# FNet mixing and gated conv FFN on one core: the order of folds and first-stage DFTs for batches 2 to 5

## The chip, the cores and the metric

The kernel runs on one core of a Trainium2 chip. The metric is the device time of one execution in microseconds, as the median of ten runs. The engines are TensorE (PE, with weight loads as PEld), VectorE (DVE), ScalarE (ACT), GpSimd (POOL) and SyncE (SP, which only issues DMAs here). Each engine works through its own queue in order; semaphores join the queues.

## The reference

Input x is (8, 3136, 256) in float32. The result feeds a gated feed-forward layer with d_ff = 1024.

```python
X = np.fft.fft(x, axis=1)
X = np.fft.fft(X, axis=2)
x = X.real                                  # (8, 3136, 256)
h = np.maximum(x @ w_in, 0.0)               # (8, 3136, 1024)
conv_out = sum(conv_w[k] * shifted(h, k - 1) for k in range(3))   # along the sequence, zero-padded
out = (h * sigmoid(conv_out)) @ w_out       # (8, 3136, 256)
```

## The kernel before

The DFT along the sequence is done per batch. First VectorE **folds** the input: sums and differences of mirrored quarters of the sequence and of mirrored features, so that a quarter of the table suffices. `fold_ops(b)` returns fourteen such operations, seven for each half `h` of a batch: `pair(0)`, `pair(2)`, `both(6)`, `feats(1)`, `both(4)`, `evens`, `feats(0)`. They work in place on a buffer `xh` (two buffers, one per half) and put their results into `wt[b]` (tiles `w`). `feats` also has a small copy and a memset on POOL. The input reaches `xh` by `load_ops`: one plain DMA and, for half 1, three tiny ones, all issued by SP, and four indirect DMAs issued by POOL for the mirrored rows. A load for a buffer waits until the last fold on that buffer is done.

Then the **first DFT** of the batch runs as eight units (`units(b)`). A unit is four matmuls of `w` with a table into one PSUM tile `pd` (`Unit.matmuls`, shown as eight matmul instructions in the profile), a copy of half of it by ScalarE (`copy`, L287 and L306; two of the units have none) and a finishing pair of VectorE operations (`fin`, L291/L294, L310/L312, L322/L324), which write the transformed batch `PQ[b]` (tiles `pt` and `qt`). There is one `pd` buffer, so a unit's first matmul waits for the pair of the unit ahead of it.

The rest is a pipeline over 256 **steps**: for each batch four chunks of the sequence, for each chunk eight blocks of 128 of the 1024 hidden features. So `per` is 32 steps for a batch. The step loop at the end of the function writes all queues by hand. In step t:

- TensorE: the two products of step t+1 into `pb` and `pa` (second DFT and `w_in` in one), then `mm2` of step t-3 with `w_out` into `po` (twelve instructions, fourteen at some steps), then what `side` holds for "pe".
- ScalarE: the sigmoid of step t-2 (L711), the copies of `pb` of step t+1 (L675), what `side` holds for "act", the seed of `pa` for step t+2 (L641), the first tap of step t (L692).
- VectorE: `combine` of step t (two of L686), what `side` holds for "dve", two taps of step t-1 (L698), the gate of step t-2 (L719, and L721 at some steps).
- POOL: its half of the gate (L718), a memset at some steps, and the loads in `side`.
- SP: the loads in `side` under "load", and the output stores, which fall due every eighth step.

`mm2` of step t-3 needs the gate that VectorE wrote in its step t-1. `combine` of step t needs the products of TensorE's step t-1.

The work on coming batches is put into steps by `at(step, where, fn)`. The list `ends` sets it: the folds of batch b are spread evenly over the steps `ends[b-1]` to `ends[b]`, and its first DFT over `ends[b]` to 32b-3. Before, `ends` is [9, 20, 46, 72, 98, 125, 157, 189]. Batch 1's DFT has nine steps (20 to 28, its last finishing pair in step 29), batch 2's fifteen, batch 3's twenty-one, batch 4's twenty-seven, the later ones thirty-two. A fold is not put where its step is in the set `taken`; that set holds the steps with a finishing pair, and two with another VectorE operation.

```python
    ends = [9] + [max(26 * b - 6, per * (b - 1) - 3) for b in range(1, B)]
...
            at(cs[i + 1], "act", u.copy)
            at(cs[i + 1], "dve", u.fin)
            taken.add(cs[i + 1])
...
        cs = [free(c0 + j * n // len(ops)) if b > 1 else c0 + j * n // len(ops) for j in range(len(ops))]
```

Finishing pairs are entered into `side` before folds, so where both fall into one step the pair comes first in VectorE's queue. When a half's last fold is placed, the loads of the next batch's same half go into the steps behind it, one operation a step.

Of the kernel before, what the change touches and what calls it, by code (L numbers as in the profile page):

```python
# [38 lines left out]
def kernel(  # L39
# [11 lines left out]
    B, S, D = x.shape  # L51
# [411 lines left out]
    def spread(b, cs):  # L463

        for c in cs:
            ch = chunks[c]
            eb[b, c] = ebp.tile([P, HN], F32, name="eb", tag="eb")[:, 0:ch.k1 - ch.k0]
            nc.sync.dma_start(out=eb[b, c], in_=ed[b:b + 1, ch.k0:ch.k1].to_broadcast([P, ch.k1 - ch.k0]))
# [322 lines left out]
    per = len(chunks) * NF  # L791
    side = {}

    def at(cycle, where, fn):
        side.setdefault((cycle, where), []).append(fn)
# [9 lines left out]
        at(NF + 1 + j // 3, "load", fn)  # L805


    ends = [9] + [max(26 * b - 6, per * (b - 1) - 3) for b in range(1, B)]
    taken = set()

    def free(cycle):

        while cycle in taken:
            cycle += 1
        taken.add(cycle)
        return cycle
# [13 lines left out]
    for b in range(1, B):  # L830
        begin, us, *_ = units(b)
        us = us[0:4] + us[5:]
        c0, n = ends[b], per * b - 3 - ends[b]
        at(max(c0, per * (b - 1) + 1), "pe", begin)
        cs = [c0 + i * n // len(us) for i in range(len(us) + 1)]
        for i, u in enumerate(us):
            k = cs[i + 1] - cs[i]
            for j in range(k):
                at(cs[i] + j, "pe", lambda u=u, j=j, k=k: u.matmuls(j, k))
            at(cs[i + 1], "act", u.copy)  # L840
            at(cs[i + 1], "dve", u.fin)
            taken.add(cs[i + 1])
        at(cs[-1] - 2, "load", lambda b=b: spread(b, range(len(chunks) - 1)))
        at(per * b + 1, "load", lambda b=b: spread(b, [len(chunks) - 1]))
    for b in range(1, B):
        ops = fold_ops(b)
        c0, n = ends[b - 1], ends[b] - ends[b - 1]
        cs = [free(c0 + j * n // len(ops)) if b > 1 else c0 + j * n // len(ops) for j in range(len(ops))]
# [107 lines left out]
```

## Time and profile before

| | us |
|---|---|
| median of ten runs | 1223.79 (1222.27 to 1224.17) |
| the profiled execution, its own time | 1223.55 |
| its span, first to last instruction | 1221.8 |

| engine | busy, us | share of the span |
|---|---|---|
| PE | 1187.1 | 97% |
| PEld | 905.4 | 74% |
| DVE | 1126.1 | 92% |
| ACT | 877.0 | 72% |
| POOL | 371.2 | 30% |

Times are microseconds unless marked ns. L719 is line 719 of the kernel. A matmul is pipelined, and its recorded end is modelled: the next one starts before it. A stage's row gives its start and end, its length, and for each engine the busy time with the number of instructions, then the granted TensorE clock, the DMA engines' busy share and GB/s. In a list of waits, a row gives who waited for whom, the sum, the count and the longest. In a timeline, a row gives start and duration, and in brackets the idle time of the engine before it with what ended it.

### The profile page before, as it was taken

The page shows a single profiled execution, that of the slowest core. Times are in us where ns is not written, and L with a number is a line of the kernel's source. Part 1 is how long each engine was busy: PE and PEld are TensorE (multiplying, and loading weights), DVE is VectorE, ACT ScalarE, POOL GpSimd, SP SyncE. Part 2 cuts the span into 40 slices and gives each one's busy share as a digit, 9 for nine tenths or more (in the row PEclk, how much of TensorE's full clock was granted, in tenths as well). Part 3 has the DMA queues.
Part 4 walks back from the last instruction along what each step waited for, and adds up shares of the span by engine and source line. Part 5 has one row for each costly group of instructions (what it writes and reads, how often), then busy time and mean ns, then how long its engine had stood idle before and what let it go on. Part 6 is the DMA issues. An engine that isn't in the chain of part 4 may idle for free.

```text
span 1221.8 us, 15450 instructions
## 1 busy us (share of the span) xinstructions
PE 1187.1 (97%) x4876; PEld 905.4 (74%) x4876; DVE 1126.1 (92%) x1696; ACT 877.0 (72%) x1832; POOL 371.2 (30%) x474
## 2 busy tenths in 40 slices
PE   5999999999999999999999999999999999999998
PEld 4676677667777777677777777777777787777776
DVE  7799978998999999999999999999998888899996
ACT  2467666777667777777776777777777777788884
POOL 5224532244142413242324242232222122222222
PEclk9999999999999999999999999999999999999999
DMA  9512231112031211211112020310001000110000
GB/s 237 178 8 80 81 48 59 54 55 75 4 99 44 73 52 33 75 53 53 53 58 61 18 79 27 86 47 26 27 1 53 31 26 27 46 33 27 26 27 31
DMA packets 70213, 66.30 MB, mean 54 GB/s; under 512 B 28123, under 2 KB 57827, under 8 KB 70131
## 3 DMA queue, kind: packets, MB, share of 16 engines
q1 hardware_dynamic: 64493, 52.18, 14.9%
q0 software_dynamic: 5120, 12.85, 3.4%
q8 instruction: 39, 0.64, 0.2%
q14 instruction: 43, 0.35, 0.1%
q10 hardware_dynamic: 518, 0.28, 0.1%
HBM read 39.53 MB, written 25.74 MB: 53 GB/s over the span
## 4 chain that ended last, share of the span: by engine, by line
PE 68%; DVE 22%; issue 4%; ACT 2%; DMA 1%; DVEq 0%; SPq 0%; ACTq 0%
PE po L94 42%; PE pb L94 10%; PE pa L94 10%; DVE g L698 7%; PE pd L94 7%; DVE h L686 4%; DVE g L719 3%; DVE xh L158 2%; DVE xh L169 1%; ACT nb L675 1%; DVE w L186 1%; DVE w L187 1%; DVE xh L173 0%; DMA xh<-in_x_dram 0%; DVE pt L291 0%
## 5 line engine op out<-in xcount | busy, mean ns | idle before, releaser
L94 PE MATMUL po<-wout,g 128*128 128x256 f32 x3072 | 709.8, 381 | 13.9 <-DVE g L719 13.3
L94 PEld LDWEIGHTS po<-wout,g 128*128 128x128 f32 x3072 | 577.9, 190 | 170.0 <-DVE g L719 50.8
L698 DVE SCALAR_TENSOR_TENSOR g<-h,cw,g 128x770 f32<-128x770 f32 (+1 forms) x512 | 549.0, 1072 | 9.3 <-ACT g L692 0.2
L718 POOL TENSOR_TENSOR g<-g,h 128x385 f32<-128x385 f32 (+1 forms) x256 | 232.5, 908 | 781.4 <-ACT g L711 520.3
L711 ACT ACTIVATE g<-g 128x385 f32<-128x385 f32 (+2 forms) x512 | 244.4, 527 | 196.8 <-DVE g L698 194.2
L675 ACT ACTIVATE nb<-pb 128x386 f32<-128x386 f32 (+2 forms) x472 | 208.2, 494 | 85.9 <-PE pb L94 85.1
L686 DVE CUSTOM_DVE_ANT_0 h<-pa,nb 128x386 f32<-128x386 f32 (+2 forms) x492 | 255.6, 560 | 3.7 <-ACT h L672 3.7
L692 ACT ACTIVATE g<-h,cw 128x770 f32<-128x770 f32 (+1 forms) x256 | 243.5, 951 | 0.1
L94 PE MATMUL pb<-qt,G 127*128 127x387 f32 (+2 forms) x512 | 212.7, 496 | 0.0
L94 PE MATMUL pa<-pt,G 128*128 128x387 f32 (+2 forms) x512 | 211.8, 494 | 0.0
L641 ACT ACTIVATE pa<-eb,ge 128x387 f32<-128x387 f32 (+2 forms) x252 | 151.7, 602 | 1.3 <-PE pa L94 0.7
L94 PEld LDWEIGHTS pa<-pt,G 128*128 128x128 f32 x512 | 96.8, 189 | 73.6 <-issue 18.2
L719 DVE TENSOR_TENSOR g<-g,h 128x385 f32<-128x385 f32 (+1 forms) x256 | 146.2, 571 | 0.9 <-ACT g L711 0.9
L94 PE MATMUL pd<-tab,w 98*128 98x196 f32 (+3 forms) x448 | 122.4, 374 | 0.0
L133 POOL DMA_INDIRECT xh<-in_x_dram,idx x64 | 106.8, 1669 | 13.4 <-issue 9.6
L94 PEld LDWEIGHTS pb<-qt,G 127*128 127x128 f32 x512 | 94.5, 190 | 17.6 <-issue 0.9
L94 PEld LDWEIGHTS pd<-tab,w 98*128 98x128 f32 (+1 forms) x448 | 83.9, 190 | 12.6
L738 ACT COPY os<-po 128x256 f32<-128x256 f32 x196 | 57.6, 394 | 8.5 <-PE po L94 4.6
L158 DVE TENSOR_TENSOR xh<-xh 98x1020 f32<-98x1020 f32 (+1 forms) x32 | 40.9, 1283 | 2.7 <-DMA xh<-in_x_dram,idx 2.5
L169 DVE TENSOR_TENSOR xh<-xh 98x1024 f32<-98x1024 f32 (+1 forms) x32 | 42.0, 1314 | 0.1
L291 DVE TENSOR_TENSOR qt<-as,pd 128x197 f32<-128x197 f32 (+1 forms) x14 | 7.2, 516 | 21.6 <-ACT as L287 21.6
L291 DVE TENSOR_TENSOR pt<-as,pd 128x197 f32<-128x197 f32 (+1 forms) x14 | 7.3, 520 | 20.2 <-ACT as L287 20.2
(114 smaller groups left out, 404.2 us busy)
## 6 DMA issues: line engine op xcount, KB each, us to landing
out_dram<-os SPq DMA_DIRECT2D x192, 128.0 KB
xh<-in_x_dram SPq DMA_DIRECT2D x16, 784.0 KB
eb<-ed SPq DMA_DIRECT2D x16, 193.5 KB
tab<-dft_seq_dram SPq DMA_DIRECT2D x4, 589.5 KB
raw<-in_moe_w_in_dram SPq DMA_DIRECT2D x4, 512.0 KB
raw<-in_moe_w_out_dram SPq DMA_DIRECT2D x1, 2048.0 KB
eb<-ed SPq DMA_DIRECT2D x8, 209.0 KB
eb<-ed SPq DMA_DIRECT2D x8, 193.0 KB
```

The costliest lines, as they stand in the source:

```text
L94: nc.tensor.matmul(o, l, r, start=start, stop=stop, skip_group_check=True)
L133: nc.gpsimd.indirect_dma_start(out=xh[b, h][0:NP, 7 - m].rearrange("p q d -> p (q d)"), out_offset=None, in_=bass.AP(tensor=x.tensor, offs ...
L158: vt(a[:, :, :, 1:D], a[:, :, :, 1:D], r[:, :, :, D - 1:0:-1], op=ALU.add)
L641: act(pa[s][:, 0:n], eb[b, c], AF.Copy, scale=ge[:, f:f + 1])
L675: act(nb[s][:, i, cols], p[:, cols], AF.Copy, scale=-1.0 if i else 1.0)
L686: nc.vector._custom_dve(TENSOR_ADD_SAT, out=to, in0=a[:, cols], in1=c[:, i, cols], s0=BIG, s1=0.0)
L692: act(gs[s], hs[s][:, 0:n], AF.Copy, scale=cw[:, 0, s[2]:s[2] + 1])
L698: stt(out=g, in0=h[:, k:k + n], scalar=cw[:, k, f:f + 1], in1=g, op0=ALU.mult, op1=ALU.add)
L711: act(gs[s][:, c], gs[s][:, c], AF.Sigmoid)
L718: gt(g[:, p], g[:, p], h[:, p], op=ALU.mult)
L719: vt(g[:, v], g[:, v], h[:, v], op=ALU.mult)
L738: nc.scalar.copy(out=osb[:, j % 2], in_=pt[:, j % 2])
```

## The change

`ends` gets other values: [9, 20, 36, 61, 93, 125, 157, 189]. The folds of batch 2 lie in steps 20 to 35, those of batch 3 in 36 to 59, those of batch 4 in 62 to 90, and those of batch 5 in 94 to 122. The first DFT of batch 2 takes steps 36 to 60, that of batch 3 steps 61 to 92, that of batch 4 steps 93 to 124. The finishing pairs of batch 1 no longer keep folds out of their steps, so that six steps from 21 to 26, and step 29, hold a pair and a fold. The loads move with the folds. `taken` is otherwise as before.

```diff
-    ends = [9] + [max(26 * b - 6, per * (b - 1) - 3) for b in range(1, B)]
+
+    ends = [9, 20, per + 4] + [per * (b - 1) - 3 for b in range(3, B)]
...
-            taken.add(cs[i + 1])
+            if b > 1:
+                taken.add(cs[i + 1])
```

## The prediction

> **What bounds the kernel now.** I read the page's busy times first, then the stages, then the waits and the timeline inside the stages that stood out.
>
> ```profile
> PE 1187.1 (97%) x4876; PEld 905.4 (74%) x4876; DVE 1126.1 (92%) x1696; ACT 877.0 (72%) x1832; POOL 371.2 (30%) x474
> PEclk9999999999999999999999999999999999999999
> ```
>
> TensorE looks full and VectorE nearly so. The granted clock is flat, so no stage is slow for that reason. But a po matmul takes 381 ns in the records while the next starts 216 ns later, so "busy" hides pauses. I therefore marked TensorE's steps by their first pb product (step 20 at 151.42 us, 28 at 196.86, 36 at 234.34, 61 at 351.75, 93 at 497.43, 125 at 642.41, 157 at 785.28, 189 at 927.69) and asked for those stretches:
>
> ```profile
> 151.42:196.86 45.44, 44.81 (x189) 34.79 (x188) 35.79 (x58) 28.63 (x60) 10.93 (x12) 1.00 0.36 62
> 196.86:234.34 37.48, 35.89 (x149) 26.08 (x149) 36.76 (x61) 26.69 (x56) 9.09 (x17) 1.00 0.11 36
> 234.34:351.75 117.41, 114.59 (x469) 87.30 (x468) 111.06 (x168) 84.29 (x175) 41.11 (x45) 1.00 0.20 60
> 351.75:497.43 145.68, 144.02 (x590) 109.89 (x589) 138.24 (x212) 107.06 (x223) 49.02 (x61) 1.00 0.18 57
> 497.43:642.41 144.98, 142.44 (x581) 108.17 (x581) 138.18 (x212) 107.41 (x223) 46.64 (x58) 1.00 0.17 55
> 642.41:785.28 142.87, 142.58 (x590) 110.37 (x589) 134.79 (x208) 108.16 (x224) 45.27 (x56) 1.00 0.16 50
> 785.28:927.69 142.41, 141.44 (x581) 108.71 (x581) 134.62 (x209) 108.30 (x224) 38.41 (x53) 1.00 0.12 38
> ```
>
> Columns: length, then busy time of PE, PEld, DVE, ACT, POOL. In the first stretch (steps 20-27) VectorE is idle for 9.65 of 45.44 us, in the second (28-35) for 0.72 of 37.48. So the bound changes from TensorE to VectorE within sixteen steps. The reason is where the folds lie. The same stretches with the instructions on xh alone:
>
> ```profile
> 151.42:196.86 45.44, 1.30 (x1) 1.00 0.36 62
> 196.86:234.34 37.48, 7.88 (x10) 1.00 0.11 36
> 234.34:351.75 117.41, 19.77 (x23) 1.00 0.20 60
> 351.75:497.43 145.68, 24.05 (x28) 1.00 0.18 57
> 497.43:642.41 144.98, 21.41 (x26) 1.00 0.17 55
> 642.41:785.28 142.87, 18.59 (x22) 1.00 0.16 50
> ```
>
> A batch's folds are 22 instructions, 18.6 us. Steps 20-27 have one of them; the stretches behind carry 23, 28 and 26. What this costs is in TensorE's wait list for steps 28 to 46 and in one step's timeline:
>
> ```profile
> PEld po L94 <- DVE g L719: 11.7, 13, 1.3
> ```
> ```profile
> 245.41 1.02 DVE L686 CUSTOM_DVE_ANT_0 h<-pa,nb 128x385 f32<-128x385 f32 x2
> 245.55 2.46 PEld L94 LDWEIGHTS po<-wout,g 128*128 128x128 f32 x12 [1.11 <-DVE g L719]
> ```
>
> TensorE has its two products out (1.30 us), then waits for the gate L719 of VectorE's step before. A VectorE step with a fold takes about 4.6 us, without one 3.4; TensorE's is 3.89 (12 po x 0.216 + 4 products x 0.325), plus a DFT's 13.3 spread over its steps. In steps 21-27 it is the other way round, VectorE waits:
>
> ```profile
> 171.10 0.33 ACT L287 COPY as<-pd 128x197 f32<-128x197 f32 x1
> 171.47 0.52 DVE L291 TENSOR_TENSOR qt<-as,pd 128x197 f32<-128x197 f32 x1 [2.76 <-ACT as L287]
> ```
>
> **The change, part by part.** The order of instructions confirms the moves; all matmuls stay. The first DFT remains in steps 20-28. Batch 2's fourteen folds go from steps 20-44 to 20-35, its DFT from 46-60 to 36-60; batch 3's folds from 46-70 to 36-59, its DFT from 72-92 to 61-92; batches 4 and 5 follow (starts 98 to 93 for DFT 4). From step 130 on nothing differs.
>
> *Steps 20-27.* Six folds (about 1.25 us each) enter steps 21-26. They stand behind the DFT's finishing pair in VectorE's queue, so the 2.76 us idle ahead of that pair are not filled; the slack behind it is what counts. Walk a step: the copy ends about 1.99 after TensorE's step begins (169.38 to 171.43 in the timeline), the pair takes 0.78, fold 1.25, two taps and gate 2.33: gate at +6.35. The next mm2 can start at 5.35 (TensorE's mean step here) + 1.30 = +6.65. That holds by 0.3. Going step by step from VectorE's 158.09 at step 21, the gates come 1.4, 1.2, 0.0, 0.1, 1.4 and 1.2 us ahead of need. Where VectorE is not waiting it has 3.38 + 0.8 + 1.25 = 5.4 to TensorE's 5.4. Cost 0.1. No row shows pair and fold in one step, so bounds: at least 0, since TensorE pauses there for only 0.9, in step 20; at most all six on the path, 6 x 1.25 = 7.5. I take 0.1, since each piece has its row.
>
> A rule speaks against this. When POOL's gate ran at 97.46-98.33, the fold begun at 97.62 took 1.780, its twin behind it 1.208. The Trainium skill (GPSIMD Engine Reference, 1. Specifications) says that POOL's SBUF interfaces are shared with VectorE, with contention for instructions that have two SBUF inputs, as each fold has. By the rule six folds grow by 0.57, 3.4 us, and with 0.3 slack a step the stretch loses about 2. By the rows at steps 36-40, also with gate and indirect loads, folds took 1.26 to 1.32; and behind the finishing pair the gate has mostly run. I keep 1.25, and 2 us in the range.
>
> *Steps 28-35.* VectorE is the bound and gets seven folds for six (the new one beside the DFT's last finishing pair): +1.3, minus 0.1 slack. Sum to step 36: +1.3.
>
> *Steps 36-60.* Folds 23 to 22 instructions, and the DFT's 13.3 us on TensorE now spread over all 25 steps. TensorE's own work is 25 x 3.89 + 13.3 + 1.3 for the wider last chunk of a batch = 111.8, so 5.6 of the 117.4 are pauses. In the two stretches that already have this layout the same sum gives 140.8 and 139.1: pauses of 2.1 and 3.3. Here the load of VectorE on TensorE is like theirs (111.1 less 1.3 for one fold is 109.8, over 111.8 is 0.98; there 134.8/140.8 and 134.6/139.1 are 0.96 and 0.97), so I take 2.9: -2.7.
>
> *Steps 61-92 and 93-124.* They become copies of 125-156 and 157-188, with equal TensorE work: 145.68 to 142.87, and 144.98 to 142.41: -2.8, -2.6. The fold time agrees: 5.5 and 2.9 us leave VectorE.
>
> A second reading of these three: the Trainium skill (Perfetto Trace Analysis, Identifying the Most-Contended Engine) wants TensorE's headroom judged by the share of weight loads, not of matmuls. Shares are 0.744, 0.754, 0.746 before, 0.773 and 0.763 in the target stretches. At 0.768, 0.773 and 0.763 they would take 113.7, 142.2 and 141.8: -10.3 instead of -8.1. I stay with the step sums, since the share also counts missing records.
>
> *Queues.* Batch 3's loads move from steps 36-50 to 27-41, batch 4's from 59-75 to 47-65, batch 5's less. On SP a load waits for the buffer's last fold (53.3 us in 8 waits, longest 13.3); behind it are stores and eb loads, due three or more steps later. POOL's indirect loads take 1.0-3.1 us each with POOL busy 10.9 of 45.4. Batch 2's second half landed at 184.8 and would be read at 197.8; later ones have nine steps. Cost nothing; if a landing slipped beyond 13 us, the fold at step 28 would pay the rest.
>
> Sum: 1.3 - 2.7 - 2.8 - 2.6 = -6.8. The profiled execution took 1223.55 (span 1221.8), so 1216.75; it lies 0.24 under the median 1223.79, so 1217.0.
>
> **Rivals.** (A) The above, 72%: with errors of about 1 in each term, 1214.5 to 1219.5.
> (B) Bunching: folds at neighbouring steps (36/37, 40/41, 43/44, two of 4.6 us) still make TensorE wait, and the rule on shared interfaces holds early: +2.5 -1.0 -2.8 -2.0 = -3.3, 1220.5. For it: L719 waits now sit at just such pairs. Against: steps 125-188 have pairs too. 12%, a third of it within 0.2% of no change, 2.45 us, which is about what a measurement of this kernel can tell.
> (C) More: steps 20-35 free, pauses of 2.1 per 32 steps everywhere: -3.9 -2.8 -3.8 = -10.5, 1213.3. Against: 28-35 has no VectorE slack. 7%.
> (D) Slower: the folds in steps 21-26 stand behind the finishing pair's wait, and that chain, not TensorE, sets the step. Then none of the idle time is usable and the moved folds are paid whole: 7 x 1.25 = 8.7, plus 6 x 0.5 of contention = 11.7, less 8.1 later: +3.6, 1227.4. It decides from about 8.1 lost in 20-35, 1.2 per fold. For it: the margin is only 0.3 a step. Against: past the margin only the excess is paid, not the fold. 7%, with 2% for a smaller such loss near no change.
>
> Faster by over 0.2%: 72 + 8 + 7 less some tail of A: 84%. Same 9%, slower 7%. The range 1213.5 to 1221.2 covers A, nearly all of B and the edge of C.
>
> **What would show it.** Right: VectorE busy near 42-43 us in steps 20-27 with that stretch's length within 0.5 of 45.4; step 36 about 1.3 later than 234.34; the PEld wait on L719 in steps 28-46 down from 11.7 to under 8; steps 61-92 and 93-124 within 1 us of 142.9 and 142.4. Wrong: L719 waits appearing in steps 21-27 (D), folds there at 1.7 us (the rule), a DMA as releaser of L158 at step 28, or pauses of 5 us staying in 36-60 (B).

## The result and the profile after

| | before | after |
|---|---|---|
| median | 1223.69 us (28 runs) | 1218.71 us (8 runs, 1217.69 to 1218.91) |
| ratio | | 0.9959, 95% interval 0.995 to 0.9967 |
| profiled execution, its span | 1223.55, 1221.8 us | 1218.81, 1217.0 us |

The change saves 5.0 us; 6.8 had been forecast. The stages of the changed kernel, cut at the same steps as before (length, then busy time of PE, PEld, DVE, ACT, POOL):

```profile
151.72:197.64 45.92, 45.08 (x190) 34.71 (x188) 42.27 (x68) 28.27 (x60) 12.93 (x16) 1.00 0.36 58
197.64:236.71 39.07, 35.98 (x149) 25.97 (x149) 38.34 (x62) 26.68 (x56) 16.45 (x21) 1.00 0.25 79
236.71:352.42 115.71, 114.58 (x469) 87.06 (x468) 110.18 (x166) 83.83 (x175) 39.24 (x44) 1.00 0.20 60
352.42:495.30 142.88, 142.59 (x589) 110.41 (x589) 134.65 (x208) 108.38 (x224) 45.96 (x56) 1.00 0.16 51
495.30:637.67 142.37, 141.41 (x582) 108.74 (x582) 134.59 (x209) 108.31 (x224) 45.40 (x57) 1.00 0.17 52
```

The instructions on xh alone, in the first three of these:

```profile
151.72:197.64 45.92, 8.88 (x11) 1.00 0.36 58
197.64:236.71 39.07, 9.09 (x11) 1.00 0.25 79
236.71:352.42 115.71, 18.58 (x22) 1.00 0.20 60
```

The folds went where the diff says: 11 instructions in each of the first two stages, 22 in the third. VectorE is busy for 42.27 us in steps 20-27, where it had been for 35.79. Against the prediction:

| steps | before | after | difference | forecast |
|---|---|---|---|---|
| 20-35 | 82.92 | 84.99 | +2.07 | +1.3 |
| 36-60 | 117.41 | 115.71 | -1.70 | -2.7 |
| 61-92 | 145.68 | 142.88 | -2.80 | -2.8 |
| 93-124 | 144.98 | 142.37 | -2.61 | -2.6 |
| sum | | | -5.04 | -6.8 |

Step 20 starts 0.30 us later in this profile, and nothing moves behind step 125, which gives the spans' -4.8. Steps 20 to 60 together won nothing (+0.37); the whole gain came from 61 to 124. TensorE's wait list for steps 28 to 46 says where the first two rows fell short:

```profile
PEld po L94 <- DVE g L719: 9.7, 11, 2.6
```

Before it was 11.7 us in 13 waits. The waits are two fewer now, but one is of 2.6 us, where the longest had been 1.3. It comes in step 30, behind the step that holds a finishing pair and a fold at once. The timeline from VectorE's step 29 on:

```profile
203.25 0.99 ACT L711 ACTIVATE g<-g 128x448 f32<-128x448 f32 x2 [1.64 <-DVE g L698]
...
204.15 0.91 ACT L675 ACTIVATE nb<-pb 128x418 f32<-128x418 f32 x2
204.94 0.32 ACT L287 COPY as<-pd 128x196 f32<-128x196 f32 x1
...
205.30 0.52 DVE L291 TENSOR_TENSOR pt<-as,pd 128x196 f32<-128x196 f32 x1 [0.48 <-ACT as L287]
...
206.00 1.22 DVE L158 TENSOR_TENSOR xh<-xh 99x1020 f32<-99x1020 f32 x1
...
209.94 0.92 PE L94 MATMUL po<-wout,g 128*128 128x256 f32 x3 [1.93 <-DVE g L719]
```

This is the chain that the prediction's walk did not have. ScalarE starts with the sigmoid, which waits for VectorE's taps (L698); then come the two copies of pb, and only then the pair's copy. TensorE's DFT unit had ended at 202.50, 2.4 us before that copy began. So when VectorE is late, ScalarE is late with it, and the pair waits for a copy that hangs on VectorE's own last step. The same in step 24:

```profile
175.78 0.94 ACT L711 ACTIVATE g<-g 128x385 f32<-128x385 f32 x2 [2.68 <-DVE g L698]
...
176.62 0.91 ACT L675 ACTIVATE nb<-pb 128x418 f32<-128x418 f32 x2
177.42 0.32 ACT L287 COPY as<-pd 128x196 f32<-128x196 f32 x1
...
177.77 0.51 DVE L291 TENSOR_TENSOR qt<-as,pd 128x196 f32<-128x196 f32 x1 [0.56 <-ACT as L287]
```

VectorE's step began at 176.21, where the gate of the step before ended, and the pair at 177.77: 1.56 us later, of which the last 0.56 were idle. Combine alone would have let it start at 1.0.

### The profile page after: what moved, and what is told of

Read it like the earlier page. It is cut to its first block, busy times and chain, and to the rows that moved or that the text cites. A ratio compares the mean times of both kernels' runs of the same rounds, so it can differ in the third digit from the quotient of the medians.

```text
span 1217.0 us, 15448 instructions
## 1 busy us (share of the span) xinstructions
PE 1185.7 (97%) x4876; PEld 906.6 (74%) x4876; DVE 1125.2 (92%) x1696; ACT 877.7 (72%) x1832; POOL 372.8 (31%) x474
## 4 chain that ended last, share of the span: by engine, by line
PE 69%; DVE 21%; issue 4%; ACT 2%; DMA 1%; DVEq 0%; SPq 0%; ACTq 0%
PE po L94 43%; PE pb L94 10%; PE pa L94 10%; DVE g L698 7%; PE pd L94 6%; DVE h L686 3%; DVE g L719 3%; DVE xh L158 2%; ACT nb L675 1%; DVE xh L169 1%; DVE w L186 1%; DVE w L187 1%; DMA xh<-in_x_dram 0%; DVE xh L173 0%; DVE pt L291 0%
## 5 line engine op out<-in xcount | busy, mean ns | idle before, releaser
L94 PE MATMUL po<-wout,g 128*128 128x256 f32 x3072 | 709.0, 380 | 11.0 <-DVE g L719 10.3
L698 DVE SCALAR_TENSOR_TENSOR g<-h,cw,g 128x770 f32<-128x770 f32 (+1 forms) x512 | 549.1, 1072 | 9.3 <-ACT g L692 0.2
L718 POOL TENSOR_TENSOR g<-g,h 128x385 f32<-128x385 f32 (+1 forms) x256 | 234.0, 914 | 767.2 <-ACT g L711 513.4
L94 PE MATMUL pd<-tab,w 98*128 98x196 f32 (+3 forms) x448 | 126.7, 374 | 0.0
L158 DVE TENSOR_TENSOR xh<-xh 98x1020 f32<-98x1020 f32 (+1 forms) x32 | 40.7, 1278 | 2.9 <-DMA xh<-in_x_dram,idx 2.9
L169 DVE TENSOR_TENSOR xh<-xh 98x1024 f32<-98x1024 f32 (+1 forms) x32 | 41.3, 1291 | 0.1
L188 POOL COPY w<-xh 98x4 f32<-98x4 f32 (+1 forms) x32 | 20.2, 632 | 28.0 <-DVE xh L169 14.8
```

The lines of the kernel that those rows point to most:

```text
L94: nc.tensor.matmul(o, l, r, start=start, stop=stop, skip_group_check=True)
L158: vt(a[:, :, :, 1:D], a[:, :, :, 1:D], r[:, :, :, D - 1:0:-1], op=ALU.add)
L698: stt(out=g, in0=h[:, k:k + n], scalar=cw[:, k, f:f + 1], in1=g, op0=ALU.mult, op1=ALU.add)
L718: gt(g[:, p], g[:, p], h[:, p], op=ALU.mult)
```

## Experiments

Theory 1: the change fell short of the forecast by this wait, 0.5 to 0.6 us on VectorE in each step where it is late and has a pair with a copy. The rival: VectorE's own work, one fold after another, sets steps 20 to 60, and the idle time is harmless. Totals are medians beside runs of the kernel before on the same chip. Profiles of kernels that are equal up to step 20 start that step anywhere from 150.28 to 152.60 us, so effects of a microsecond are read from the stages.

**One part alone.** The kernel before, with batch 1's pairs no longer in `taken`:

```diff
-            taken.add(cs[i + 1])
+            if b > 1:
+                taken.add(cs[i + 1])
```

> The kernel before with one part of the change: batch 1's finishing pairs no longer keep folds out of their steps; the list ends stays as before. Batch 2's folds then lie in steps 20 to 44 (nine up to step 34, not seven, and five in 36 to 44, not seven); all from step 46 on is as before. Theory 1 (a finishing pair waits behind ScalarE's sigmoid and pb copies, about 0.6 us on VectorE in each step that has both): steps 20-35 about 0.5 to 1 us longer, steps 36-45 (43.9 us before) down to about 40.5, together -2 to -3 us, 1221. Rival (VectorE's own work alone sets these steps): the same folds are done in the same steps 20-45, so only the evenness counts, -3 us or more, as nothing is lost in 20-35.

Measured: 1219.95 us, ratio 0.9969 (0.9958 to 0.9981). Steps 20-35 took 83.1 us (+0.2), steps 36-45 40.4 (-3.5); steps 36-60 113.9. So this line alone wins 3.3 us in steps 20-60, where the full change wins nothing. The -3.3 and the +0.2 lie nearer to the rival (-3 or more, nothing lost in 20-35) than to theory 1 (-2 to -3, with 0.5 to 1 lost there); by themselves they don't decide. What the run shows is that steps 20-60 get shorter where fourteen folds are spread over 25 steps, and not where they are put into sixteen.

**The early copy.** On the changed kernel, for all batches:

```diff
-            at(cs[i + 1], "act", u.copy)
+            at(cs[i + 1], "act0", u.copy)
...
             sigmoid(steps[t - 2])
+        run("act0")
         if t + 1 < n:
             products(steps[t + 1])
```

> The changed kernel, with ScalarE's copy for the finishing pair put right behind the sigmoid, ahead of the two copies of pb, for all batches. Theory 1: the pair's copy then ends about 0.85 us after VectorE's step begins, not 1.7, so VectorE no longer idles 0.6 us in each step with a pair in which it is late. Steps 20-35 go from 85.0 back to about 83.3, steps 36-60 lose 0.5 to 1: total -2 to -3 us against the changed kernel, about 1216. Rival (VectorE's own work alone sets the steps): within 0.5 us of the changed kernel, as no operation is taken off VectorE. A second rival: the pb copies come 0.35 us later and hold up VectorE's combine, +1 us or more.

Measured: 1206.76 us, ratio 0.9865 (0.985 to 0.988): 12 us less than the changed kernel. The first rival and the second are out; but the theory's own figure, 2 to 3 us, was four to six times too small. The stages:

```profile
151.41:196.85 45.44, 44.81 (x190) 34.80 (x188) 44.05 (x72) 29.92 (x62) 13.37 (x17) 1.00 0.37 61
196.85:233.51 36.66, 35.62 (x149) 26.15 (x149) 36.41 (x58) 26.04 (x54) 16.06 (x21) 1.00 0.26 81
233.51:347.55 114.04, 113.28 (x470) 87.69 (x469) 111.10 (x168) 85.57 (x176) 39.13 (x44) 1.00 0.20 61
347.55:489.20 141.65, 141.65 (x589) 110.66 (x589) 136.76 (x207) 109.68 (x224) 47.57 (x57) 1.00 0.16 51
489.20:629.16 139.96, 139.96 (x582) 109.19 (x582) 136.83 (x208) 108.81 (x223) 47.96 (x57) 1.00 0.17 53
```

Steps 20-35 fall from 84.99 to 82.10 (about 83.3 was expected), 36-60 from 115.71 to 114.04 (0.5 to 1 was expected). What I had not seen is that the stretches used as models of a good layout carried the same wait: 61-92 and 93-124 get shorter by another 1.2 and 2.4 us, and so do 125-156 and 157-188. VectorE's waits for the copies, and TensorE's for the gate, in steps 61-124 of the changed kernel (twelve pairs with a copy, twelve waits):

```profile
DVE qt L291 <- ACT as L287: 6.0, 4, 1.6
DVE pt L291 <- ACT as L287: 4.9, 4, 1.6
DVE as L310 <- ACT as L306: 2.7, 4, 0.9
PEld po L94 <- DVE g L719: 9.0, 18, 1.1
```

With the early copy, in the same steps:

```profile
DVE qt L291 <- ACT as L287: 1.8, 2, 0.9
DVE as L310 <- ACT as L306: 0.6, 1, 0.6
```

TensorE no longer waits for a gate there, and its records show no idle time: PE busy equals the length. Step 24 with the early copy:

```profile
173.92 0.94 ACT L711 ACTIVATE g<-g 128x385 f32<-128x385 f32 x2 [1.36 <-DVE g L698]
...
174.97 0.32 ACT L287 COPY as<-pd 128x196 f32<-128x196 f32 x1
...
175.32 0.51 DVE L291 TENSOR_TENSOR qt<-as,pd 128x196 f32<-128x196 f32 x1
...
175.67 0.93 ACT L675 ACTIVATE nb<-pb 128x418 f32<-128x418 f32 x2 [0.38 <-PE pb L94]
```

The pair starts 0.96 us after VectorE's step does (174.36), straight behind combine, with no idle time in its row. VectorE's waits in steps 21 to 29, all of them, first of the changed kernel, then with the early copy:

```profile
DVE qt L291 <- ACT as L287: 1.7, 2, 1.2
DVE as L310 <- ACT as L306: 1.1, 2, 0.6
DVE pt L291 <- ACT as L287: 1.0, 2, 0.5
```
```profile
DVE pt L322 <- PE pd L94: 0.9, 1, 0.9
```

The pb copies, put back by the pair's copy, cost nothing that shows: in this step they wait 0.38 us for TensorE anyway. The longest of the waits that are gone, 1.17 us, was in step 23, where VectorE had been early: there the pair's copy stood behind pb copies that waited for TensorE's products. So the wait came from ScalarE's order in both cases, with VectorE late and with VectorE early.

**Fold ahead of the pair.** On the changed kernel, ScalarE untouched:

```diff
-            at(cs[j], "dve", fn)
+            at(cs[j], "dve0" if b == 2 else "dve", fn)
...
+        run("dve0")
         run("dve")
```

> The changed kernel, with batch 2's folds put ahead of batch 1's finishing pair in VectorE's queue where both are in one step (21 to 26 and 29); ScalarE as it is. Theory 1: the fold fills the wait for the copy, VectorE's idle time in steps 21-29 (4.0 us) falls below 1.5, but the pair releases the PSUM tile about 1.25 us later, so TensorE's next DFT unit waits up to 0.5 us in a step where VectorE is late: steps 20-35 83.5 to 85 (85.0 now), -0 to -1.5 us. Rival (VectorE's own work alone): no change within 0.3 us. If the release of the tile weighs more than the wait, slower by 1 us or more.

Measured: 1216.79 us, ratio 0.9947 (0.9933 to 0.996). Steps 20-35 took 83.5 us, 1.5 less; all stages behind are as in the changed kernel to 0.03 us. VectorE does the same work, so the rival (no change) is out: an idle gap that a fold can fill was costing time. VectorE's waits in steps 21-29 went from 3.8 to 2.2 us, not below 1.5 as expected; 1.8 of what is left is in step 27, which has no fold. The 83.5 is the low end of what was expected, so no loss by the later release of the PSUM tile shows.

**The later part undone.**

```diff
-    ends = [9, 20, per + 4] + [per * (b - 1) - 3 for b in range(3, B)]
+    ends = [9, 20, 36] + [max(26 * b - 6, per * (b - 1) - 3) for b in range(3, B)]
```

> The changed kernel with the later part undone: ends is 9, 20, 36, 72, 98, 125, so batch 2's folds and DFT lie as in the changed kernel, batch 3's folds spread over steps 36 to 71 and its DFT in 72 to 92, batches 4 and 5 as before. Prediction's sums: steps 20-35 as in the changed kernel (85.0), 36-60 about 1 us shorter than there (ten folds, not fourteen), 61-92 near halfway between before and changed (144.3), 93-124 as before (145.0). Total about 1221.5, so that the later part is worth 2.5 to 3 us. Rival (the later stretches recover by themselves, and the gain lies in step 20 to 60): 1219, same as the changed kernel.

Measured: 1220.43 us, ratio 0.9974 (0.9965 to 0.9983). Steps 20-35 85.0, 36-60 114.3, 61-92 143.8, 93-124 145.0. Three of the four came as said, and 61-92 half a microsecond better. The stretches don't recover by themselves: the later part takes 0.9 and 2.6 us off steps 61-124 and costs 1.4 in 36-60, so it is worth 2.1 by the stages, 1.7 by the medians, less than the 2.5 to 3 expected.

**The early copy without the change**, on the kernel before:

> The kernel before, with the early copy alone. It tells what the change is worth when the finishing pairs don't wait. Theory 1 (two separate losses: pairs waiting behind ScalarE, and folds bunched on few steps): steps 125-188 fall to the early copy's work bound (141.7 and 140.0), 61-92 and 93-124 to about 142.5 and 141, while steps 36-45, which have seven folds and no DFT, stay at 43.9: about 1212, so the change is worth 5 us with the early copy as without it. Rival (one loss: the change helped only because its layout has fewer late pairs): about 1207, as with change and early copy together.

Measured: 1211.89 us, ratio 0.9905 (0.9888 to 0.9921). Steps 36-60 and the two behind:

```profile
231.82:349.22 117.40, 114.58 (x469) 87.32 (x468) 111.82 (x170) 85.25 (x176) 41.62 (x46) 1.00 0.20 62
349.22:491.74 142.52, 142.12 (x589) 110.55 (x589) 139.30 (x209) 107.10 (x221) 49.46 (x61) 1.00 0.18 57
491.74:634.23 142.49, 141.05 (x582) 108.84 (x581) 138.76 (x214) 108.90 (x224) 47.78 (x58) 1.00 0.17 56
```

Steps 36-60 are as long as before (117.40 against 117.41): their loss is in 36-45, which took 43.90 us as before, with seven folds and no DFT. So there are two separate losses, and the rival of a single one (about 1207 us) is out. With the early copy the change is worth 5.1 us by medians (1211.89 to 1206.76), as much as without it, but in other places: steps 20-35 +1.2, 36-60 -3.4, 61-92 -0.9, 93-124 -2.5. Expected for 93-124 was 141; it stayed at 142.5. Pairs wait for copies there for 1.8 us in two waits, while TensorE still waits for the gate for 4.7 us in seven; folds on neighbouring steps are the likely reason, which no run isolates.

**The one line and the early copy.**

> Batch 2's folds allowed into the first DFT's steps, the list ends as before, and the early copy. Expected from the stretches measured: steps 20-35 about 82.3, 36-60 113.0, 61-92 142, 93-124 140.5: 1206, level with change and early copy (1206.8). If the longer lists of the change are needed, 1208 or more.

Measured: 1207.72 us, ratio 0.9865 (0.9849 to 0.9882). Steps 20-60 took 194.8 us, 1.3 less than with the whole change (196.1), but 61-92 and 93-124 took 142.5 and 142.4, 0.9 and 2.5 more. Expected there were 142 and 140.5. By the stages this kernel is 2.1 us behind change and early copy, by the medians 1.0, with step 20 starting 1.2 us later in its profile. The longer lists of the change are needed for the later batches.

**One size altered**, change and early copy:

```diff
-    ends = [9, 20, per + 4] + [per * (b - 1) - 3 for b in range(3, B)]
+    ends = [9, 20, 40, 66, 95] + [per * (b - 1) - 3 for b in range(5, B)]
```

> The change and the early copy with one size altered: ends is 9, 20, 40, 66, 95, 125, so that batch 2's folds have twenty steps and not sixteen, batch 3's twenty-six. If what is left of the pauses in steps 28-40 (2.4 and 1.8 us) comes from a run of steps with a fold each (VectorE 4.6 against TensorE 3.9 to 4.3 us), about half of it goes: 1204.5. If steps 20-60 are bounded by the sum of VectorE's work, no change within 0.5 us: 1206.8.

Measured: 1207.33 us, ratio 0.9866 (0.9849 to 0.9882), no gain. Steps 20-35 82.1, 36-60 114.2, as with the shorter list. In its profile steps 30, 31 and 33 to 35 still hold a fold each, and 32 a feature operation of 1.2 us: the longer list thinned the folds mostly in steps 23, 26 and 29, and not in the run behind them. So this does not settle whether the rest of the pauses in steps 28-40 comes from that run or from the sum of the work.

**Both remedies.**

> The change with the early copy and with the fold ahead of the pair. Theory 1: with the early copy there is no wait left for the fold to fill, so the order of the two does nothing, or it costs up to 1 us by the later release of the PSUM tile: 1206.8 to 1207.8. Rival (the gain of fold first came from somewhere else): another 1.5 us less, 1205.2.

Measured: 1205.80 us, ratio 0.9853 (0.9837 to 0.987), the fastest of all. But from step 20 on its profile is level with that of the early copy (steps 20-35 82.0 and 82.1, all others to 0.01); the difference lies ahead of step 20, where the two kernels are equal. The total alone would speak for the rival (1205.2); the stages speak for theory 1: with the wait gone the order of fold and pair does nothing.

**The early copy for batch 1 alone**, to size the wrong term where it stood:

```diff
-            at(cs[i + 1], "act", u.copy)
+            at(cs[i + 1], "act0" if b == 1 else "act", u.copy)
```

> The changed kernel, with the early copy for batch 1's DFT alone (steps 21 to 29), to size the wrong term of the prediction where it stood. If the excess of steps 20-35 over the prediction is the pairs' wait behind ScalarE, these steps go from 85.0 to 82.1 us as with the early copy everywhere, and all behind stays as in the changed kernel (115.7, 142.9, 142.4): 1215.8. If the early copy's gain in steps 20-35 hung on later steps, less than 1 us of it appears: over 1217.8.

Measured: 1214.87 us, ratio 0.9934 (0.9921 to 0.9948).

```profile
150.72:196.16 45.44, 44.81 (x189) 34.80 (x188) 44.05 (x72) 29.90 (x62) 13.34 (x17) 1.00 0.38 60
196.16:232.82 36.66, 35.63 (x150) 26.16 (x149) 36.41 (x58) 26.03 (x54) 16.04 (x21) 1.00 0.28 82
232.82:348.52 115.70, 114.60 (x470) 87.09 (x469) 110.14 (x166) 83.83 (x175) 39.24 (x44) 1.00 0.20 60
```

Steps 20-35 take 82.10, as named, and 36-60 stay at 115.70. The effect is local. (The total fell by 0.9 more than by these 2.9; in its profile step 20 starts 1.0 us earlier, and the kernel before, beside it on another chip, was at 1223.22.)

**Two copies**, the suspected wait made longer:

```diff
             at(cs[i + 1], "act", u.copy)
+            at(cs[i + 1], "act", u.copy)
```

> The changed kernel with each of the finishing pairs' copies done twice, one behind the other, in the late place. ScalarE has 0.33 us more in six steps of a batch and is busy for 72% of the span. Theory 1: each late pair waits 0.33 us longer; over the 42 steps with such a copy (seven batches) that is at most 13.9 us, and by the early copy's ratio (0.85 us earlier gave 12 us) about +4.6: 1223. Rival (the early copy helped not by the pair's wait but by what it did to the order of the sigmoid and pb copies): ScalarE has room, so within 1 us of the changed kernel: 1218.7.

Measured: 1224.27 us, 5.6 more than the changed kernel; ratio to the kernel before 1.0007 (0.9998 to 1.0016). The later stages, steps 36-60, 61-92 and 93-124:

```profile
237.46:354.32 116.86, 115.23 (x470) 86.71 (x468) 110.17 (x166) 84.98 (x180) 37.24 (x44) 1.00 0.19 60
354.32:498.00 143.68, 143.01 (x589) 110.07 (x589) 134.54 (x208) 109.77 (x230) 46.21 (x56) 1.00 0.16 50
498.00:641.31 143.31, 141.86 (x581) 108.42 (x581) 134.57 (x209) 109.84 (x230) 45.44 (x57) 1.00 0.16 52
```

Every stage with a DFT grew, by 1.1, 1.2, 0.8 and 0.9 us for steps 20-35, 36-60, 61-92 and 93-124. VectorE's busy time did not (134.54 against 134.65 us in 61-92), and ScalarE is idle for a quarter of each. The waits of steps 61-124 are those shown above, grown by 1.9 and by 3.7 us:

```profile
DVE qt L291 <- ACT as L287: 6.6, 4, 1.8
DVE pt L291 <- ACT as L287: 5.4, 4, 1.6
DVE as L310 <- ACT as L306: 3.5, 4, 1.0
PEld po L94 <- DVE g L719: 12.7, 21, 1.1
```

The rival named above, that the order of the sigmoid and the pb copies had helped and not the pair's wait, is out: that order is as in the changed kernel here. The second copy also puts back the seed and the first tap, but no wait on either shows in these steps. A third of a microsecond on an engine with room cost as much as the whole change had won.

## Why the prediction was right, and where it was off

- *What bounds the kernel.* Right as far as it went: TensorE's steps wait for the gate of a VectorE step that carries a fold. But the wait of a pair behind ScalarE's queue was seen only where VectorE is early, and taken as harmless; it was the larger loss, 12 us with the change, against 5 for the place of the folds.
- *Steps 61-92 and 93-124 become copies of later stretches.* Right to 0.04 us (142.88 and 142.37 against 142.87 and 142.41). Reading the length of a target layout that stands in the same trace gave the best terms of the sum.
- *Steps 20-35, +1.3: short by 0.8.* The failing step is the walk through 21-27, in the clause "the copy ends about 1.99 after TensorE's step begins". That was read off step 23, where VectorE is early and waits. Where VectorE is late, the copy's time counts from VectorE: the sigmoid waits for its taps, and the copy for the sigmoid and the pb copies. The walk let the pair start right behind combine there, at about +1.0 (its 3.38 less the 2.33 of taps and gate); the trace shows 1.56. The gate for TensorE's step 25, forecast to be ready 0.1 us before need, came 0.4 late, and the wait of step 30 grew from 0.6 to 2.1, most of it the fold that the forecast had charged. With the early copy the walk is right: steps 20-27 take 45.44, as before the change, and 28-35 are 1.2 longer with the change than without (36.66 against 35.45; I had +1.2). Two readings in the walk are also off, by little: the copy in step 23 ends 2.05 after the step begins (169.38 to 171.43), not 1.99, and 5.35 is the mean of steps 22, 23, 24 and 26, while that of steps 20-27 is 5.68.
- *Steps 36-60, -2.7: short by 1.0.* The term mis-sized is the pauses, taken as 2.9 from the model stretches and in fact 3.9 (115.71 less the prediction's 111.8 of TensorE's work). This stretch starts behind a run of folds, with VectorE late. The early copy brings the pauses to 2.2, so the pairs' waits are 1.7 of the 3.9. All of that lies in steps 46-60; 36-45 take 46.25 us with either copy, an estimated 1.5 over TensorE's work there (44.75, the usual start-to-start times of its matmuls in the early-copy trace added up).
- *The model stretches.* I took what they had left, 2.1 and 3.3 us, as what such a layout costs. It was the same wait: with the early copy 0.9 is left of each by that sum, and as the records show no idle time there, this is work that the sum left out (it falls short alike in every such stretch, so the differences stand). The weight-load shares had hinted at more room, and the 113.7 us worked out from them for steps 36-60 is near what the early copy reached (114.0), not the change. That one is partly luck: their other two figures, 142.2 and 141.8, lie above its 141.65 and 139.96 (and the three together make -10.4, not -10.3).
- *Shared SBUF interfaces.* The rule that the prediction cites cost next to nothing in these steps, because folds and POOL's gate hardly met. Folds L158 of the changed kernel in steps 20 to 47, minimum, median and maximum in ns:

```profile
L158 DVE TENSOR_TENSOR xh<-xh x6: 1211/1240/1305, 154.6 to 244.1; 98x1020 f32<-98x1020 f32 x4, 99x1020 f32<-99x1020 f32 x2
```

  None took the 1.78 us of step 9; I charged 1.25. Over both traces the time of a fold on L158 or L169 follows its overlap with the gate (L718): up to 0.10 us of overlap it takes 1.20 to 1.23, with 0.17 to 0.24 it takes 1.25 to 1.33, with 0.37 it takes 1.45, with 0.65 to 0.72 it takes 1.73 to 1.80. (One fold at 270.86 is left out, where the gate's own record is 2.87 us long.) So the rule and the rows at steps 36-40, which the prediction set against each other, agree: the fold loses most of the overlap, and behind the finishing pair little is left of the gate. The 2 us kept in the range were not needed.
- *Queues and loads.* Right at no cost: no fold on line 158, the first to read a load, waited for a DMA in these steps.
- *Rival B*, bunching, can't be told from the forecast by the first two rows: its +2.5 and -1.0 are as near to the measured +2.07 and -1.70 as the forecast's +1.3 and -2.7. Its early loss by shared interfaces was not there. Its bunching may be: of the 1.5 us left in steps 36-45 with the early copy, most is in steps 36 to 38, where mm2 starts 2.0, 1.5 and 1.6 us into the step in place of 1.3, and folds stand in 36 and 37. No run isolates it.
- *The signs.* VectorE's busy time in steps 20-27 and the lengths of 61-92 and 93-124 came as named. The length of 20-27 did not quite (45.92, where within 0.5 of 45.4 was named), step 36 started 2.4 us later and not 1.3, and the waits for the gate in steps 28-46 fell to 9.7 us and not under 8. One sign against came in small: two waits for the gate in steps 21-27, 1.2 us in all, where there had been none.
- *The total* lies in the range because the two later rows were right and the two early ones, short by 0.8 and 1.0 in the same direction, stayed within the error that had been allowed. That they did was luck as far as the walk goes, since the wait that it left out had no term.
- *Rival D*, idle time not usable behind the pair's wait, was right in mechanism and wrong in size. The wait is real, but past the margin only the excess is paid: steps 20-35 lost 2.1 us, not 11.7.

## What to carry to other kernels

When work is moved into a step beside a dependent pair, follow the operand of that pair through the queue of the engine that makes it, for the case that the receiving engine is late as well as for the case that it is early: an operand that stands behind work on the late engine's own product costs its wait every time (0.5 to 0.6 us here). An engine with a quarter of its time idle can still set the pace by the order of its queue; an edit of two lines that moved a 0.32 us copy ahead of two others, in 42 steps, was worth 12 us, more than the layout change it was meant to explain. A stretch that already has the target layout is the best forecast of a term, but its leftover pauses are a finding to be explained, not a constant.

## What the runs showed of the hardware that was not expected

TensorE's weight loads fill 0.78 of a stretch in which its records show no idle time (110.66 of 141.65 us, 109.19 of 139.96), so a share of 0.75 to 0.77, as in steps 61-188 before, is within about 5% of that pace. A fold's time follows its overlap with POOL's gate, from 1.21 us with none to 1.78 with 0.70 us of it. And the part of the program ahead of step 20, which no edit here touches, differed by up to 2.3 us between profiles (step 20 at 150.28 to 152.60 us), as much as half of what the change moved; the cause was not looked for.
